# Transposing k and q by DMA instead of on TensorE, from the sixth slot on, in a linear-attention kernel fused with a bilinear FFN

## The chip, the core and the metric

The kernel runs on one core of a Trainium2 chip. The core has TensorE (PE, with its weight loads shown apart as PEld), VectorE (DVE), ScalarE (ACT), GpSimd (POOL) and SyncE (SP); each engine works through its own list of instructions in order, and 16 DMA engines serve the transfers that SP and ACT issue. The metric is the device time of one execution in microseconds (us), less is better.

## What is computed

q, k and v are 4 batches x 8 heads x 768 positions x 64 (float32). A state of 64 x 64 for each head is decayed by gamma and gets the outer product of k and v at each position; y is q times the state. Then y, laid out as 3072 tokens x 512, goes through a bilinear feed-forward layer with three weights of 512 x 1536, 512 x 1536 and 1536 x 512.

```python
for t in range(S):
    state = gamma[None, :, None, None] * state + np.einsum('bhd,bhe->bhde', k[:, :, t], v[:, :, t])
    y[:, :, t] = scale * np.einsum('bhd,bhde->bhe', q[:, :, t], state)
...
a = x @ w_a
b = x @ w_b
return (a * b @ w_out).astype(np.float32)
```

## The kernel before, in words

**Slots.** The 3072 tokens are 24 slots of 128 (4 batches x 6 chunks). The recurrence is done in its chunked form: within a slot as masked attention, between the slots of a batch by a state that PE accumulates in PSUM. A slot passes through these steps:

- `load_slot` (line 81): three DMAs from SP, 256 KB each, for k, q and v in float32. The buffers `kf`, `qf`, `vf` are six deep. Weights are loaded by `load_w` and `load_o` (768 KB each) from the same queue. `LOADS` (line 19) is the order of all loads; the first five are issued at once, the rest in line 306.
- `casts` (line 166): k is multiplied by a decay table into `kb` (bf16), q into `qb`, v is cast to `vb`. From slot 3 on all three run on POOL. These buffers are six deep too.
- `step_a` (line 178): eight PE transposes of 128 x 128 (lines 181 and 183) put k and q into one PSUM tile, and a DVE copy (line 185) brings them to SBUF as `kqT`, three deep.
- `step_b` (line 187): eight matmuls `at` (line 193) from `kqT`, the mask on DVE (line 197, into `aT`), the state update `st` (line 203), and two ACT copies of the state.
- `step_c` (line 212): the output `y` of the slot, from the state and `kqT` (line 218) and from `vb` and `aT` (line 223), copied by ACT into `xt` (line 228).

**FFN.** Slots are grouped in seven tiles J of 3, 2, 4, 4, 4, 4 and 3 slots. `ffn_ab` (line 246) makes one of twelve blocks of the hidden layer of a tile: four matmuls `a` (line 253), an ACT cast, four matmuls `g` (line 259), and a product on DVE (line 261). `ffn_out` (line 263) makes the 128 x 512 output of one slot with twelve matmuls `o` (line 266), an ACT copy, and a store issued from the ACT queue.

**Order.** `seq` (line 70) chains every instruction to the one before on its engine, so that the order in the code is the order on each engine. `run` (line 273) lays the steps of the next tile between the FFN pieces of this one, at positions that are given as a list, in the order a, (c of the slot before), b; it issues the casts of a slot up to four pieces ahead. The first FFN tile starts when slots 0 to 2 are through. During J=1, slots 5 to 8 are done: the pieces are the last six `ffn_ab` of J=1, then the three `ffn_out` of J=0 and two of J=1, and the positions (line 317) put step a of slot 5 before the fourth of these pieces and step b of slot 5 before the fifth.

**Waits of DMAs.** The transfers use eight semaphores in turn: a DMA issue waits for the transfer that used its semaphore last, so no more than eight are under way at a time, stores of the ACT queue among them. An issue waits in its queue, and what stands behind it waits too.

Of the kernel before, what the change touches and what calls it, by code (L numbers as in the profile page):

```python
# [10 lines left out]
BF16 = mybir.dt.bfloat16  # L11
# [6 lines left out]

LOADS = ("s0 s1 s2 w0 w1 s3 w2 s4 w3 o0 o1 o2 o3 "
         + " ".join(f"s{t}" for t in range(5, 24))).split()  # L20


@with_exitstack
def kernel(
# [10 lines left out]
    nc = tc.nc  # L35
    P = 128
    B, H, S, D = q.shape
    NCH = S // P
    HP = H // 2
# [4 lines left out]
    NSLOT = B * NCH  # L44
# [9 lines left out]
    wstage = ctx.enter_context(tc.tile_pool(name="wstage", bufs=4))  # L54
    raw = ctx.enter_context(tc.tile_pool(name="raw", bufs=6))
    nat = ctx.enter_context(tc.tile_pool(name="nat", bufs=6))
    tra = ctx.enter_context(tc.tile_pool(name="tra", bufs=3))
    xtp = ctx.enter_context(tc.tile_pool(name="xtp", bufs=2))
    asbp = ctx.enter_context(tc.tile_pool(name="asbp", bufs=3))
    htp = ctx.enter_context(tc.tile_pool(name="htp", bufs=2))  # L60
# [9 lines left out]
    def seq(bi):  # L70
        ins = bi.ins
        prev = last.get(ins.engine)
        if prev is not None:
            tc.add_manual_dep(ins, prev.name, nosync, reason="program order")
        last[ins.engine] = ins
        return bi
# [25 lines left out]
    pending = list(LOADS)  # L102

    def issue_loads(n):
        for _ in range(min(n, len(pending))):
            what = pending.pop(0)
            {"s": load_slot, "w": load_w, "o": load_o}[what[0]](int(what[1:]))
# [33 lines left out]
    def cast(engine, dst, src):  # L141
        if engine is nc.scalar:
            seq(nc.scalar.copy(dst, src))  # L143
        else:
            seq(engine.tensor_copy(dst, src))  # L145
# [10 lines left out]
    kb, qb, vb, kqT, aT = {}, {}, {}, {}, {}  # L156
# [9 lines left out]
    def casts(t):  # L166
        ci = t % NCH
        early = t < TILES[0]
        kb[t] = nat.tile([P, H, D], BF16, tag="kb", name="kb")
        qb[t] = nat.tile([P, H, D], BF16, tag="qb", name="qb")  # L170
        vb[t] = nat.tile([P, H, D], BF16, tag="vb", name="vb")
        seq((nc.vector if early else nc.gpsimd).tensor_tensor(  # L172
            kb[t], raws["k", t], ktab[:, ci, :, :].to_broadcast([P, H, D]), op=ALU.mult))
        seq(nc.gpsimd.tensor_tensor(  # L174
            qb[t], raws["q", t], qtab[:, ci, :, :].to_broadcast([P, H, D]), op=ALU.mult))
        cast(nc.scalar if early else nc.gpsimd, vb[t], raws["v", t])

    def step_a(t):
        tp = psat.tile([P, 2, HP, P], BF16, tag="at", name="tp")
        for hp in range(HP):  # L180
            seq(nc.tensor.transpose(tp[:, 0, hp, :], kb[t][:, 2 * hp : 2 * hp + 2, :], ident))  # L181
        for hp in range(HP):
            seq(nc.tensor.transpose(tp[:, 1, hp, :], qb[t][:, 2 * hp : 2 * hp + 2, :], ident))  # L183
        kqT[t] = tra.tile([P, 2, HP, P], BF16, tag="kqT", name="kqT")
        seq(nc.vector.tensor_copy(kqT[t], tp))  # L185

    def step_b(t):
# [24 lines left out]
    def step_c(t):  # L212
        ci = t % NCH
        J, i = where[t]
        y = psat.tile([P, HP, P], F32, tag="at", name="y")
        if ci > 0:
            for hp in range(HP):
                seq(nc.tensor.matmul(y[:, hp, :], gst[t % 2][:, hp, :], kqT[t][:, 1, hp, :],  # L218
                                     start=(hp == 0), stop=False, skip_group_check=True))
        for hp in range(HP):  # L220
            for e in range(2):
                r = slice(64 * e, 64 * e + 64)
                seq(nc.tensor.matmul(y[r, hp, :], vb[t][:, 2 * hp + e, :], aT[t][:, e, hp, :],  # L223
                                     start=(ci == 0 and hp == 0), stop=(hp == HP - 1),
                                     skip_group_check=True))
        if i == 0:
            xt[J] = xtp.tile([P, KT, 4 * P], BF16, tag="xt", name="xt")
        seq(nc.scalar.copy(xt[J][:, :, i * P : (i + 1) * P], y))  # L228

    def steps(slots):  # L230

        slots = list(slots)
        todo = []
        for i in range(len(slots) + 1):
            if i < len(slots):
                todo.append((step_a, slots[i]))
            if i > 0:
                todo.append((step_c, slots[i - 1]))
            if i < len(slots):
                todo.append((step_b, slots[i]))  # L240
        return todo
# [32 lines left out]
    def run(work, todo, at, ahead=4):  # L274

        order = []
        for g, w in enumerate(work):
            order += [todo[i] for i in range(len(todo)) if at[i] == g]
            order.append(w)
        starts = [s for fn, s in todo if fn is step_a]  # L280
        for i, (fn, *args) in enumerate(order):
            for fn2, *a2 in order[i : i + ahead + 1]:
                if fn2 is step_a and a2[0] in starts:
                    starts.remove(a2[0])
                    casts(a2[0])
            fn(*args)

    def ab0(ft):
# [4 lines left out]
    casts(0)  # L293
    casts(1)
    step_a(0)
    casts(2)
    step_b(0)
    step_a(1)
    step_c(0)
    step_b(1)  # L300
# [2 lines left out]
    step_b(2)  # L303
    cast_w(0)
    step_c(2)
    issue_loads(100)

    work = [(ab0, ft) for ft in range(NFT)] + [(ffn_ab, 1, ft) for ft in range(6)]
    todo = steps([3, 4])
    run(work, todo, [6, 7, 9, 10, 11, 12], ahead=3)  # L310
    for j in range(NW):
        cast_o(j)
    work = [(ffn_ab, 1, ft) for ft in range(6, NFT)]
    work += [(ffn_out, 0, i) for i in range(TILES[0])]
    work += [(ffn_out, 1, i) for i in range(TILES[1])]
    todo = steps(range(5, 9))
    run(work, todo, [3, 4, 5, 6, 6, 7, 7, 8, 8, 9, 9, 10])
    slot = sum(TILES[:3])
    for J in range(2, len(TILES)):
        n = TILES[J]  # L320
        nxt = range(slot, slot + TILES[J + 1]) if J + 1 < len(TILES) else range(0)
        slot += len(nxt)
        todo = steps(nxt)
        work = [(ffn_ab, J, ft) for ft in range(NFT)] + [(ffn_out, J, i) for i in range(n)]
        run(work, todo, [i * (len(work) - 1) // len(todo) for i in range(len(todo))])
# [30 lines left out]
```

## Time and profile before

| | us |
|---|---|
| median of 3 runs (255.37 to 256.64) | 256.04 |
| the profiled execution, its time | 255.94 |
| its span in the trace | 254.2 |
| PE busy | 233.5 |
| DVE busy | 102.2 |
| ACT busy | 91.6 |
| POOL busy | 73.6 |
| loads on the SP queue, share of 16 DMA engines | 50.1% |
| stores on the ACT queue, share of 16 DMA engines | 6.7% |

The span is 1.7 us shorter than the time of that execution; a change of the span is taken to change the time by as much. The profile has a view of the span in 40 slices, a chain of work that ended last (from the last instruction back to whatever released each piece), groups of instructions by line, DMA issues with their time to landing, and the order of instructions in time. In the chain a matmul counts only until the next one starts, so that its times add up; in the groups the durations of matmuls overlap.

### The profile page before, as it was taken

The page shows a single profiled execution, that of the slowest core. Times are in us where ns is not written, and L with a number is a line of the kernel's source. Part 1 is how long each engine was busy: PE and PEld are TensorE (multiplying, and loading weights), DVE is VectorE, ACT ScalarE, POOL GpSimd, SP SyncE. Part 2 cuts the span into 40 slices and gives each one's busy share as a digit, 9 for nine tenths or more (in the row PEclk, how much of TensorE's full clock was granted, in tenths as well). Part 3 has the DMA queues.
Part 4 walks back from the last instruction along what each step waited for, and adds up shares of the span by engine and source line. Part 5 has one row for each costly group of instructions (what it writes and reads, how often), then busy time and mean ns, then how long its engine had stood idle before and what let it go on. Part 6 is the DMA issues. An engine that isn't in the chain of part 4 may idle for free.

```text
span 254.2 us, 4303 instructions
## 1 busy us (share of the span) xinstructions
PE 233.5 (92%) x1672; PEld 127.0 (50%) x1696; DVE 102.2 (40%) x173; ACT 91.6 (36%) x179; POOL 73.6 (29%) x84
## 2 busy tenths in 40 slices
PE   0487889899999999999999999999999999999994
PEld 0363445786555455445455445445445454446641
DVE  1462375465325456305455306455205465104410
ACT  2154233534243442423434412444314333223311
POOL 5115474286757667503133403000000000000000
PEclk9999999999999999999999999999999999999999
DMA  7999997999999999969910021000021000120012
GB/s 155 219 358 289 303 292 257 296 217 205 252 239 271 209 214 220 191 173 274 183 32 3 3 112 55 0 0 3 24 100 44 0 0 3 41 97 27 3 41 84
DMA packets 84181, 34.88 MB, mean 137 GB/s; under 512 B 75457, under 2 KB 79553, under 8 KB 84161
## 3 DMA queue, kind: packets, MB, share of 16 engines
q1 hardware_dynamic: 80704, 28.32, 50.1%
q10 hardware_dynamic: 3456, 6.29, 6.7%
q8 instruction: 13, 0.21, 0.4%
q14 instruction: 8, 0.06, 0.1%
HBM read 28.31 MB, written 6.29 MB: 136 GB/s over the span
## 4 chain that ended last, share of the span: by engine, by line
PE 88%; SPq 3%; DMA 2%; ACT 2%; DVE 2%; issue 2%; DVEq 0%; ACTq 0%
PE g L259 25%; PE a L253 25%; PE o L266 24%; PE y L223 3%; PE at L193 3%; SPq L86 3%; PE st L203 3%; DMA vf<-in_v_dram 2%; PE tp L181 2%; PE tp L183 2%; PE y L218 2%; DVE wb_bf L145 1%; ACT gst L210 1%; ACT wa_bf L143 1%; ACT xt L228 0%
## 5 line engine op out<-in xcount | busy, mean ns | idle before, releaser
L261 DVE TENSOR_TENSOR ht<-g,asb 128x512 bf16<-128x512 f32 (+2 forms) x84 | 51.6, 615 | 86.8 <-PE g L259 69.2
L253 PE MATMUL a<-xt,wa_bf 128*128 128x512 bf16 (+2 forms) x325 | 76.6, 354 | 2.7 <-ACT xt L228 2.3
L259 PE MATMUL g<-xt,wb_bf 128*128 128x512 bf16 (+2 forms) x332 | 76.5, 353 | 2.6 <-DVE wb_bf L145 2.5
L256 ACT CAST asb<-a 128x512 bf16<-128x512 f32 (+2 forms) x84 | 44.0, 524 | 70.6 <-PE a L253 56.1
L266 PE MATMUL o<-wo_bf,ht 128*128 128x512 bf16 x279 | 63.5, 379 | 0.6 <-issue 0.2
L259 PEld LDWEIGHTS <-wb_bf 128*128 128x128 bf16 x336 | 33.0, 99 | 33.5 <-DVE wb_bf L145 3.6
L266 PEld LDWEIGHTS <-ht 128*128 128x128 bf16 x288 | 27.4, 98 | 31.6
L253 PEld LDWEIGHTS <-wa_bf 128*128 128x128 bf16 x336 | 30.7, 99 | 24.6 <-issue 2.7
L197 DVE TENSOR_TENSOR aT<-at,mask 128x512 bf16<-128x512 f32 x48 | 30.7, 681 | 7.0 <-PE at L193 7.0
L172 POOL TENSOR_TENSOR kb<-kf,ktab 128x512 bf16<-128x512 f32 x21 | 21.9, 1042 | 37.0 <-DMA kf<-in_k_dram 16.7
L185 DVE COPY kqT<-tp 128x1024 bf16<-128x1024 bf16 x24 | 16.4, 683 | 38.4 <-PE tp L183 38.4
L269 ACT COPY osb<-o 128x512 f32<-128x512 f32 x24 | 14.0, 585 | 46.7 <-PE o L266 36.7
L174 POOL TENSOR_TENSOR qb<-qf,qtab 128x512 bf16<-128x512 f32 x24 | 25.0, 1042 | 11.7 <-DMA qf<-in_q_dram 11.2
L210 ACT CAST gst<-st 64x256 bf16<-64x256 f32 x40 | 14.6, 366 | 15.5 <-PE st L203 15.1
L228 ACT CAST xt<-y 128x512 bf16<-128x512 f32 x24 | 14.0, 585 | 15.9 <-PE y L223 13.4
L145 POOL CAST vb<-vf 128x512 bf16<-128x512 f32 x21 | 13.5, 644 | 20.9 <-issue 14.9
L181 PE MATMUL tp<-ident,kb 128*128 128x128 bf16 x96 | 10.0, 230 | 5.0 <-DVE kb L172 5.0
L223 PE MATMUL y<-aT,vb 128*64 128x128 bf16 x192 | 11.1, 235 | 2.1 <-DVE aT L197 2.1
L193 PE MATMUL at<-kqT 64*128 64x128 bf16 x192 | 10.2, 230 | 2.5 <-DVE kqT L185 2.0
L181 PEld LDWEIGHTS <-kb 128*128 128x128 bf16 x96 | 7.7, 103 | 9.1 <-DVE kb L172 5.0
L193 PEld LDWEIGHTS <-kqT 64*128 64x128 bf16 x192 | 5.8, 98 | 10.5 <-issue 7.1
L183 PE MATMUL tp<-ident,qb 128*128 128x128 bf16 x96 | 10.0, 231 | 0.9 <-POOL qb L174 0.9
(28 smaller groups left out, 68.0 us busy)
## 6 DMA issues: line engine op xcount, KB each, us to landing
kf<-in_k_dram SPq DMA_DIRECT2D x24, 256.0 KB, 5.1
qf<-in_q_dram SPq DMA_DIRECT2D x24, 256.0 KB, 5.1
vf<-in_v_dram SPq DMA_DIRECT2D x24, 256.0 KB, 5.1
out_dram<-osb ACTq DMA_DIRECT2D x24, 256.0 KB, 2.1
wsta<-in_moe_w_a_dram SPq DMA_DIRECT2D x4, 768.0 KB, 6.5
wstb<-in_moe_w_b_dram SPq DMA_DIRECT2D x4, 768.0 KB, 7.6
wsto<-in_moe_w_out_dram SPq DMA_DIRECT2D x4, 768.0 KB, 7.3
```

Of the source, the lines that this page charges most:

```text
L172: seq((nc.vector if early else nc.gpsimd).tensor_tensor(kb[t], raws["k", t], ktab[:, ci, :, :].to_broadcast([P, H, D]), op=ALU.mult))
L174: seq(nc.gpsimd.tensor_tensor(qb[t], raws["q", t], qtab[:, ci, :, :].to_broadcast([P, H, D]), op=ALU.mult))
L181: seq(nc.tensor.transpose(tp[:, 0, hp, :], kb[t][:, 2 * hp : 2 * hp + 2, :], ident))
L193: seq(nc.tensor.matmul(at[e][:, hp, :], kqT[t][r, 0, hp, :], kqT[t][r, 1, hp, :], start=True, stop=True))
L197: seq(nc.vector.tensor_tensor(aT[t][:, e], at[e], mask, op=ALU.mult))
L210: seq(nc.scalar.copy(g[r, :, r], st[r, :, r]))
L223: seq(nc.tensor.matmul(y[r, hp, :], vb[t][:, 2 * hp + e, :], aT[t][:, e, hp, :], start=(ci == 0 and hp == 0), stop=(hp == HP - 1), skip_gr ...
L253: seq(nc.tensor.matmul(a, wa_bf[:, kt, fs], xt[J][:, kt, :w], start=(kt == 0), stop=(kt == KT - 1)))
L256: seq(nc.scalar.copy(asb, a))
L259: seq(nc.tensor.matmul(g, wb_bf[:, kt, fs], xt[J][:, kt, :w], start=(kt == 0), stop=(kt == KT - 1)))
L261: seq(nc.vector.tensor_tensor(ht[J][:, ft, :w], g, asb, op=ALU.mult))
L266: seq(nc.tensor.matmul(o, ht[J][:, ft, i * P : (i + 1) * P], wo_bf[:, ft, :], start=(ft == 0), stop=(ft == NFT - 1)))
```

## The change

`step_a` of slots 5 to 23 no longer transposes on PE. It issues two DMA transposes from the SP queue, one from `kb` and one from `qb`, straight into the two halves of `kqT`: bf16, 128 x 512 each, 128 KB. The PE transposes, the PSUM tile and the DVE copy of these slots go. Slots 0 to 4 stay as they were. The buffers `kqT` and `aT` become four deep. The slot loads are no longer all issued in line 306: those of slots 9 to 23 are held back, and one slot's load is issued with the casts of each slot from 5 on.

In the program this gives the following order on the SP queue after the weights. L5 stands for the three loads of slot 5, T5 for its two transposes: L5 L6 L7 L8 L9 L10 T5 T6 L11 L12 T7 T8 L13 L14 T9 T10 L15 T11 L16 T12 L17 L18 T13 T14 L19 T15 L20 T16 L21 L22 T17 T18 L23 T19 T20 T21 T22 T23. Each T of k waits for the cast of k and for the last reader of its `kqT` buffer, which is step c of the slot four before; each T waits for the cast that makes its source. The first matmul of step b waits for both T of its slot.

```diff
+DMA_FROM = 5
...
-    tra = ctx.enter_context(tc.tile_pool(name="tra", bufs=3))
+    tra = ctx.enter_context(tc.tile_pool(name="tra", bufs=4))
...
     def step_a(t):
+        kqT[t] = tra.tile([P, 2, HP, P], BF16, tag="kqT", name="kqT")
+        if t >= DMA_FROM:
+            for i, src in enumerate((kb[t], qb[t])):
+                seq(nc.sync.dma_start_transpose(kqT[t][:, i], src.rearrange("p h d -> p (h d)")))
+            return
         tp = psat.tile([P, 2, HP, P], BF16, tag="at", name="tp")
         for hp in range(HP):
             seq(nc.tensor.transpose(tp[:, 0, hp, :], kb[t][:, 2 * hp : 2 * hp + 2, :], ident))
         for hp in range(HP):
             seq(nc.tensor.transpose(tp[:, 1, hp, :], qb[t][:, 2 * hp : 2 * hp + 2, :], ident))
-        kqT[t] = tra.tile([P, 2, HP, P], BF16, tag="kqT", name="kqT")
         seq(nc.vector.tensor_copy(kqT[t], tp))
...
                 if fn2 is step_a and a2[0] in starts:
                     starts.remove(a2[0])
                     casts(a2[0])
+                    if a2[0] >= DMA_FROM:
+                        issue_loads(1)
...
-    issue_loads(100)
+    issue_loads(len(pending) - (NSLOT - 9))
```

## The prediction

> **What bounds the kernel now.** I read the page's head, the slices and the chain first.
>
> ```profile
> span 254.2 us, 4303 instructions
> ...
> PE 233.5 (92%) x1672; PEld 127.0 (50%) x1696; DVE 102.2 (40%) x173; ACT 91.6 (36%) x179; POOL 73.6 (29%) x84
> ...
> DMA  7999997999999999969910021000021000120012
> ...
> PE 88%; SPq 3%; DMA 2%; ACT 2%; DVE 2%; issue 2%; DVEq 0%; ACTq 0%
> ```
>
> PE is the bound: 88% of the chain. But for the first 20 slices (6.36 us each, so until about 127 us) the DMA engines are as full as PE. Two limits lie side by side there, and the change moves work from one to the other. So the stage to look at is where slots 5 to 8 pass, 52 to 80 us. The chain of that stretch (start, duration, what):
>
> ```profile
> 55.12 0.22 PE tp L181 x4
> 55.34 0.22 PE tp L183 x4
> 55.57 0.44 PE a L253 x4
> 56.00 0.44 PE g L259 x4
> 56.44 0.33 PE at L193 x8
> ...
> 66.37 0.33 PE at L193 x8
> ...
> 77.60 0.86 PE a L253 x4
> ...
> 79.33 0.33 PE at L193 x8
> ```
>
> A slot's eight transposes hold PE for 0.22 + 0.22 = 0.44 us. Step b of slots 5, 7 and 9 (the `at` rows) starts at 56.44, 66.37 and 79.33, and tile J=2 begins at 77.60. PE has no gap here. The loads for these slots, from the SP queue's order in time (start, length of the issue), and POOL's casts:
>
> ```profile
> 50.61 0.94 SPq L86 DMA_DIRECT2D kf<-in_k_dram  x1
> ...
> 61.76 1.07 SPq L86 DMA_DIRECT2D kf<-in_k_dram  x1
> ...
> 68.51 0.88 SPq L86 DMA_DIRECT2D vf<-in_v_dram  x1
> ```
>
> ```profile
> 53.18 1.04 POOL L174 TENSOR_TENSOR qb<-qf,qtab 128x512 bf16<-128x512 f32 x1
> ...
> 64.43 1.04 POOL L174 TENSOR_TENSOR qb<-qf,qtab 128x512 bf16<-128x512 f32 x1
> ...
> 70.72 1.04 POOL L172 TENSOR_TENSOR kb<-kf,ktab 128x512 bf16<-128x512 f32 x1 [0.40 <-PE y L223]
> ```
>
> From slot 6's k (50.61) to slot 9's k (61.76) nine loads are issued, 1.24 us each: this is the pace of a full queue. Slot 5's q is cast by 54.2, slot 8's q is cast at 64.43, slot 10's k at 70.72, each soon after it landed. So before, slots 5 to 8 get their data just in time, with PE transposing within about a microsecond of the cast.
>
> **What the change removes.** 19 slots x 0.44 us = 8.4 us from PE, all on the chain. It also takes 19 copies of 683 ns from DVE; DVE is 40% busy and waits for PE, so that is worth nothing. The fourth `kqT`/`aT` buffer costs nothing.
>
> **What it adds: T5 stands behind the loads of slots 9 and 10.** Step b of slot 5 needs T5, at 56.44 - 0.44 = 56.0. T5 comes after L10 in the queue. First bound, the issue: T5 of k waits for the semaphore last used by the eighth transfer before it, slot 8's q, in use until about 64.4 (its cast); T5 of q waits for slot 8's v (cast at 65.5). So they can't even be issued before 64 and 65.5. Second, the engines: if the transfers of one queue are served in order, T5 moves after L10. Slot 10's k lands at about 70.6, q and v follow at 1.2 each: 73.0. Then two transposes, x each. T5 is there at 73.0 + 2x.
>
> **What is x?** No row shows a DMA transpose. From below: 128 KB at the 250 GB/s of this stage is 0.5 us. Next, a whole load's pace, 1.2 us, for twice the bytes. Next, a store, the only transfer out of SBUF that the trace has, lands in 2.1 us; that is x if transposes don't overlap each other. From above, a load's landing in the full queue, 5.1 us.
>
> ```profile
> kf<-in_k_dram SPq DMA_DIRECT2D x24, 256.0 KB, 5.1
> ...
> out_dram<-osb ACTq DMA_DIRECT2D x24, 256.0 KB, 2.1
> ```
>
> A transpose scatters each source row over all partitions, so I take no less than a load, and between 1.2 and 2.1 the nearer side of the load: **x = 1.5**. Both ends, 0.5 and 5.1, stay for the range.
>
> [...]
>
> **The sum at x = 1.5.**
> 1. T5 at 76.0 against 56.0: PE stands for 20.0 us in front of step b of slot 5. Nothing hides it: all that follows on PE, the `ffn_out` of J=0 too, stands behind that matmul.
> 2. After such a stop PE starts slowly. At the first FFN tile, after little work on PE, the first 16 matmuls take 1.44 + 3 x 1.28 = 5.3 us, where four soon take 0.65 (2.6 for 16). I charge 2.7 us, though the granted clock is 1.00 in these windows and I can't say that the same will come.
>
> ```profile
> 21.54 1.44 PE a L253 x4
> 22.98 1.28 PE g L259 x4
> 24.26 1.28 PE a L253 x4
> 25.54 1.28 PE g L259 x4
> ...
> 31.33 0.65 PE g L259 x4
> ```
>
> 3. T7 comes after T6, L11, L12: T5 + 2x + 6 x 1.2 + 2x and 0.7 for a store between (6.7% of 254.2 us over 24 stores), T5 + 13.9. Step b of slot 7 is wanted at T5 + (66.37 - 56.44) - 0.88 (two slots' transposes) + 2.7 = T5 + 11.75. 2.15 us are lost. T6, at T5 + 3.0, is early enough: step b of slot 6 is due at T5 + 5.5.
> 4. T9 comes after T8, L13, L14: T5 + 13.9 + 3.0 + 7.2 + 3.0 + 2.8 (four stores) = T5 + 29.9. Step b of slot 9 is wanted at T5 + 13.9 + (79.33 - 66.37) - 0.88 = T5 + 26.0. 3.9 us are lost.
> 5. From there the queue gains: a slot costs DMA 3.0 + 3.7 + 0.7 = 7.4 us, and PE about 9.4 (tile J=3 begins at 115.35 in the chain, 37.7 us after J=2, four slots). T(t) waits for step c of slot t-4, about three slots, 28 us, ahead of its use; the loads behind it in the queue are ten slots ahead. Stores share the eight semaphores, so an ACT store can wait for a transpose, and ACT's copies behind it; with this lead it doesn't. I charge nothing; were DMA slower than PE per slot (x above 2.5), this cover is gone.
>
> Together 20.0 + 2.7 + 2.15 + 3.9 - 8.4 = +20.35: 255.94 + 20.35 = 276.3, **276 us** (the median of the runs is 0.1 above the profiled execution; I add nothing).
>
> By the same steps x = 0.5 gives 18.0 + 2.7 - 8.4 = +12.3, 268; x = 2.4 gives 21.8 + 2.7 + 5.75 + 7.5 - 8.4 = +29.35, 285.
>
> **Rivals.**
> - *Transposes are the bound* (x of 2.5 to 5.1). For it: scattered small pieces. Against: half the bytes of a load. At x = 3 the steps give 291 (slot 6 is late by 0.5 as well), and each of some ten slots costs 1.0 more than PE takes: about 301. At 5.1 DMA is the bound to the end: 38 x 5.1 + 13 slots' loads at 3.7 + 16 stores at 0.7 = 253 after 73.0, and 40 us from the last `at` (213.9) to the end: a span of 366, 368.
> - *Transposes overtake the loads.* If T5 is bound by its issue alone, it lands some 2 us (a store's landing) after 65.5, at 67.5: 11.5 - 8.4 = +3.1 without the slow start, +5.8 with it: 259 to 262. Against it: the loads of one queue land in order throughout.
> - *The other side: faster.* The stop at slot 5 is cheaper than 8.4 us. With the slow start the turn is at T5 = 56.0 + 8.4 - 2.7 = 61.7. For that the 18 loads from 45.2 on would have to be through by about 60, 0.8 us each instead of 1.24, and the issue's bound of 64 would have to fall. With no stop left it gives 255.94 - 8.4 = 247.5. Speaking for it: weight loads in the slices before run at up to 358 GB/s. Against it: where slot loads make the traffic, the windows from 46 to 115 us show 212 to 255.
> - *The change doesn't do what it says*: the transposes stay. Not so: the program has 304 fewer rows on PE, 19 x 16 transposes with their weight loads.
>
> **Chances.** T5 behind the loads, x up to 2.5 (264 to 287): 0.64, and 276 is near its middle. Transposes as the bound, above 287: 0.20. Overtaking, 258 to 264: 0.08. Faster by over 0.5% (about what a measurement can tell): 0.05. Within 0.5%: 0.03. The range takes in the case of the early T5's upper end and the slow transposes up to x = 3 and a little: 262 to 305. The further tail to 368 stays out.
>
> **What would show it.** A gap of about 20 us on PE before the first `at` of slot 5, released by DMA, from 56 on; the DMA slices full through it; step a's rows 96 - 76 = 20 left in each of its two groups; smaller gaps before slots 7 and 9, none later; the transposes' landing time. The forecast is wrong if T5 lands well before slot 10's v, or if gaps before `at` recur in every slot to the end.

## The result, and the profile after

The changed kernel takes 270.87 us (median of 4 runs, 270.1 to 271.21) against 256.34 (4 runs of the kernel before, 255.37 to 257.11): a ratio of 1.056, 95% interval 1.052 to 1.059. The forecast was 276, range 262 to 305. The profiled execution took 270.68 us, 14.7 more than that of before. The page of the changed kernel first: the engines, the slices, and the first DMA queue (packets, MB, share of 16 engines).

```profile
span 269.0 us, 4032 instructions
...
PE 227.8 (85%) x1523; PEld 119.4 (44%) x1544; DVE 90.3 (34%) x154; ACT 91.7 (34%) x179; POOL 72.7 (27%) x84
...
PE   1487888910096999999999999999999999999994
...
PEclk9997999995579799999999999999999999999999
DMA  8999997999999999998999474211021100020002
...
q1 hardware_dynamic: 101376, 33.30, 59.8%
```

PE does less (227.8 us against 233.5) and the span is longer. The hole is in slices 9 to 11 of the PE row, 54 to 74 us, with the DMA row full beneath it, and the granted clock (PEclk) falls in the same place. From the queue's row the price of a transpose can be had: (59.8% of 269.0 - 50.1% of 254.2) / 38 = 0.88 us of packet time on all 16 engines. Who waited on PE from 54 us on, in the view of waits (total, times, longest):

```profile
PE at L201 <- DMA kqT<-qb: 20.5, 2, 18.4
```

Two waits for a transpose, in front of step b of slots 5 and 7, and none after. In PE's order in time (start, length, in brackets the idle time before and its releaser):

```profile
53.97 0.60 PE L261 MATMUL a<-xt,wa_bf 128*128 128x256 bf16 x4
54.41 0.60 PE L267 MATMUL g<-xt,wb_bf 128*128 128x256 bf16 x4
73.36 0.61 PE L201 MATMUL at<-kqT 64*128 64x128 bf16 x8 [18.35 <-DMA kqT<-qb]
...
86.41 0.40 PE L201 MATMUL at<-kqT 64*128 64x128 bf16 x8 [2.16 <-DMA kqT<-qb]
```

And SP's order in time shows why T5 is so late: its casts were done by 54.5, but it is issued at 68.4, right behind the last load of slot 10, and the loads in front of it go out one by one, some 1.2 us apart.

```profile
67.16 1.14 SPq L90 DMA_DIRECT2D vf<-in_v_dram  x1
68.41 1.76 SPq L186 DMA_TRANSPOSE kqT<-kb  x1
70.27 1.21 SPq L186 DMA_TRANSPOSE kqT<-qb  x1
```

In the chain tile J=2 begins at 98.49 in place of 77.60, 20.9 us late:

```profile
98.49 0.86 PE a L261 x4
```

From there to the end the span is 6.1 us shorter than before: 14 slots x 0.44 = 6.2.

### The profile page after: what moved, and what is told of

It reads as the page before. It is cut to its first block, busy times and chain, and to the rows that moved or that the text cites. A ratio compares the mean times of both kernels' runs of the same rounds, so it can differ in the third digit from the quotient of the medians.

```text
span 269.0 us, 4032 instructions
## 1 busy us (share of the span) xinstructions
PE 227.8 (85%) x1523; PEld 119.4 (44%) x1544; DVE 90.3 (34%) x154; ACT 91.7 (34%) x179; POOL 72.7 (27%) x84
## 3 DMA queue, kind: packets, MB, share of 16 engines
q1 hardware_dynamic: 101376, 33.30, 59.8%
## 4 chain that ended last, share of the span: by engine, by line
PE 63%; SPq 16%; DMA 13%; issue 2%; ACT 2%; POOL 2%; ACTq 0%; POOLq 0%
PE o L274 19%; PE a L261 18%; PE g L267 18%; SPq L90 14%; DMA vf<-in_v_dram 5%; DMA wsto<-in_moe_w_out_dram 4%; PE y L231 2%; PE at L201 2%; PE st L211 2%; DMA qf<-in_q_dram 2%; DMA kf<-in_k_dram 2%; DMA kqT<-qb 1%; PE y L226 1%; SPq L97 1%; SPq L186 1%
## 5 line engine op out<-in xcount | busy, mean ns | idle before, releaser
L267 PE MATMUL g<-xt,wb_bf 128*128 128x512 bf16 (+2 forms) x334 | 77.6, 356 | 2.6 <-DVE wb_bf L149 2.4
L274 PE MATMUL o<-wo_bf,ht 128*128 128x512 bf16 x279 | 65.4, 386 | 0.7 <-issue 0.4
L261 PEld LDWEIGHTS <-wa_bf 128*128 128x128 bf16 x336 | 31.6, 100 | 28.5 <-issue 2.4
L176 POOL TENSOR_TENSOR kb<-kf,ktab 128x512 bf16<-128x512 f32 x21 | 21.9, 1042 | 43.9 <-DMA kf<-in_k_dram 26.1
L201 PE MATMUL at<-kqT 64*128 64x128 bf16 x192 | 10.4, 233 | 22.6 <-DMA kqT<-qb 20.5
L178 POOL TENSOR_TENSOR qb<-qf,qtab 128x512 bf16<-128x512 f32 x24 | 25.6, 1065 | 9.2 <-DMA qf<-in_q_dram 7.6
L149 POOL CAST vb<-vf 128x512 bf16<-128x512 f32 x21 | 12.8, 611 | 34.1 <-PE y L231 14.6
L218 ACT CAST gst<-st 64x256 bf16<-64x256 f32 x40 | 14.7, 367 | 15.8 <-PE st L211 15.4
L231 PE MATMUL y<-aT,vb 128*64 128x128 bf16 x192 | 10.9, 232 | 2.1 <-DVE aT L205 2.1
L231 PEld LDWEIGHTS <-vb 128*64 128x64 bf16 x192 | 6.6, 113 | 6.1 <-issue 4.2
L211 PE MATMUL st<-vb,kb 128*128 128x128 bf16 x80 | 8.6, 234 | 0.5 <-ACT gst L218 0.5
L226 PEld LDWEIGHTS <-gst 128*128 128x128 bf16 x80 | 6.5, 103 | 3.9
L226 PE MATMUL y<-kqT,gst 128*128 128x128 bf16 x80 | 8.2, 228 | 0.0
## 6 DMA issues: line engine op xcount, KB each, us to landing
kf<-in_k_dram SPq DMA_DIRECT2D x24, 256.0 KB, 4.8
qf<-in_q_dram SPq DMA_DIRECT2D x24, 256.0 KB, 5.0
vf<-in_v_dram SPq DMA_DIRECT2D x24, 256.0 KB, 5.1
out_dram<-osb ACTq DMA_DIRECT2D x24, 256.0 KB, 2.2
```

Source lines behind the costliest of these rows:

```text
L176: seq((nc.vector if early else nc.gpsimd).tensor_tensor(kb[t], raws["k", t], ktab[:, ci, :, :].to_broadcast([P, H, D]), op=ALU.mult))
L178: seq(nc.gpsimd.tensor_tensor(qb[t], raws["q", t], qtab[:, ci, :, :].to_broadcast([P, H, D]), op=ALU.mult))
L201: seq(nc.tensor.matmul(at[e][:, hp, :], kqT[t][r, 0, hp, :], kqT[t][r, 1, hp, :], start=True, stop=True))
L261: seq(nc.tensor.matmul(a, wa_bf[:, kt, fs], xt[J][:, kt, :w], start=(kt == 0), stop=(kt == KT - 1)))
L267: seq(nc.tensor.matmul(g, wb_bf[:, kt, fs], xt[J][:, kt, :w], start=(kt == 0), stop=(kt == KT - 1)))
L274: seq(nc.tensor.matmul(o, ht[J][:, ft, i * P : (i + 1) * P], wo_bf[:, ft, :], start=(ft == 0), stop=(ft == NFT - 1)))
```

## The experiments

The theory is called "place in the queue": all of the loss comes from where T5 to T8 stand in SP's order, behind loads that nobody needs yet. The rivals: transposes are too dear for the full DMA engines; they are late wherever they stand; the loads that are held back are late. Every run is compared with the kernel before, timed beside it (255.9 to 256.4).

### 1. Transposes from slot 9 on, each behind the next load only

```diff
-DMA_FROM = 5
+DMA_FROM = 9
...
                 seq(nc.sync.dma_start_transpose(kqT[t][:, i], src.rearrange("p h d -> p (h d)")))
+            issue_loads(1)
             return
...
-                    if a2[0] >= DMA_FROM:
-                        issue_loads(1)
...
-    issue_loads(len(pending) - (NSLOT - 9))
+    issue_loads(len(pending) - (NSLOT - 11))
```

> Slots 5 to 8 go back to TensorE, slots 9 to 23 stay with DMA; each transpose stands in the queue behind the load of the next slot only (L9 L10 T9 L11 T10 L12 T11 ...). Theory 'place in the queue': the loss is the two stops in front of slots 5 and 7, because T5 stands behind L10 and T7 behind L12. Here T9 is there at about 74.5 + 1.8 = 76.3 us, before its use at 79, and no stop is left: 255.9 - 15 x 0.44 = 249.3 us, PE with no wait for a transpose over 0.5 us. Rival 'the engines can't take it' (transposes cost DMA time that the loads need, until 130 us): T9 to T12 run in the same full queue as T5 to T8 did, so stops of some us come back in J=2: 256 us or more. Rival 'late whatever the place': a transpose takes too long from cast to use, 255 or more.

Measured: 249.29 us (4 runs, 249.06 to 249.38), ratio 0.974 (0.973 to 0.976). This is the best kernel of the study, 2.6% faster than the one before and 8% faster than the changed one. All PE waits from 60 us to the end, and SP's rows around T9:

```profile
PE o L275 <- issue: 0.2, 1, 0.2
```

```profile
68.15 0.72 SPq L90 DMA_DIRECT2D vf<-in_v_dram  x1
71.94 1.28 SPq L186 DMA_TRANSPOSE kqT<-kb  x1
73.33 1.21 SPq L186 DMA_TRANSPOSE kqT<-qb  x1
```

T9 is issued by 74.5; step b of slot 9 starts at 79.04 and waits for nothing. The gain is 6.65 us, 15 x 0.44. The DMA engines were about as full here in J=2 as in the changed kernel's stop (DMA share 1.10 from 74 to 112 us against 1.13 from 54 to 74; it is the sum of the packets' times over 16 engines' time, and packets overlap, so it can pass 1). So both rivals fall as they were put: the transposes of slots 9 to 23 stood early enough in this run, and PE waited for none of them in the full stage.

### 2. T5 three slot loads earlier

```diff
-    issue_loads(len(pending) - (NSLOT - 9))
+    issue_loads(len(pending) - (NSLOT - 6))
```

> The changed kernel with one number altered: loads are held back from slot 6 on, not 9, so that T5 stands behind L7, three slot loads earlier (L5 L6 L7 T5 T6 L8 L9 T7 T8 L10 L11 T9 ...). 'Place in the queue': three loads are 11.1 us, T5 lands at 73.3 - 11.1 = 62.2, the first stop falls from 18.4 to about 7 us, and the time by about 11 us, to 260. 'The engines can't take it' and 'late whatever the place': the first stop stays within 3 us of 18 and the time at 268 to 271.

Measured: 259.0 us (2 runs, 258.86 and 259.13). PE's rows with an idle time in front of a step b:

```profile
61.97 0.61 PE L201 MATMUL at<-kqT 64*128 64x128 bf16 x8 [6.12 <-DMA kqT<-qb]
74.74 0.40 PE L201 MATMUL at<-kqT 64*128 64x128 bf16 x8 [1.13 <-DMA kqT<-qb]
...
88.14 0.40 PE L201 MATMUL at<-kqT 64*128 64x128 bf16 x8 [1.28 <-DMA kqT<-qb]
```

The first stop falls from 18.35 to 6.12 us, T5 comes 11.4 us earlier, and the time falls by 11.9. One number moves the loss as the theory says. Small stops remain in front of slots 7 and 9; T5 still stands behind L6 and L7.

### 3. Only slots 5 to 8 by DMA

```diff
-        if t >= DMA_FROM:
+        if DMA_FROM <= t < 9:
```

> Only slots 5 to 8 are transposed by DMA, 9 to 23 on TensorE, the order of the loads as in the changed kernel. 'Place in the queue': all of the loss sits in slots 5 to 8 and each later slot only gained 0.44 us, so the time rises by 15 x 0.44 = 6.6 us to 277.5, with the two stops of 18.4 and 2.2 us unchanged. Rival 'the later transposes cost too': without them the time falls below 270.9.

Measured: 275.1 us (274.82 and 275.38). The two stops were not unchanged but 16.65 and 1.45 us, 2.4 us less than in the changed kernel:

```profile
72.71 0.61 PE L201 MATMUL at<-kqT 64*128 64x128 bf16 x8 [16.65 <-DMA kqT<-qb]
...
85.46 0.40 PE L201 MATMUL at<-kqT 64*128 64x128 bf16 x8 [1.45 <-DMA kqT<-qb]
```

270.87 + 6.6 - 2.4 = 275.1. That this comes out so well is partly luck: PE reached slot 5 about 1.0 us later here (56.1 against 55.0), and after the shorter second stop the granted clock stayed at 1.00, which saves the 1.7 us of a second slow start; the two pull opposite ways. Even so, slots 9 to 23 earned their 0.44 us each in the changed kernel too, and the loss is in slots 5 to 8.

### 4. Only the hold-back of the loads

```diff
-        if t >= DMA_FROM:
+        if t >= NSLOT:
```

> No DMA transpose at all: TensorE transposes every slot, but the slot loads are held back and the buffers are four deep as in the changed kernel. 'Place in the queue' holds that the hold-back alone costs nothing, since the loads keep their order and run ten slots ahead: within 0.5% of 256. Rival 'the loads are late': over 258, with POOL waiting for slot loads and PE for POOL.

Measured: 256.0 us (10 runs, 255.19 to 256.43), ratio 0.9999 (0.9985 to 1.0013). Holding the loads back, and the fourth buffers, cost nothing by themselves that these runs could tell.

### 5. Slots 5 to 8 from the ACT queue

Run 3 with one word changed.

```diff
-                seq(nc.sync.dma_start_transpose(kqT[t][:, i], src.rearrange("p h d -> p (h d)")))
+                seq(nc.scalar.dma_start_transpose(kqT[t][:, i], src.rearrange("p h d -> p (h d)")))
```

> Only slots 5 to 8 by DMA, as in the run that had only these, but issued from the ACT queue in place of the SP queue; so they stand behind no load, while the 16 DMA engines carry the same bytes. 'Place in the queue': T5 is issued right after the cast of slot 5's q (54.4 us), lands 3 to 4 us later at 58 to 59, and the first stop falls from 17 to 3 or 4 us. The later ones may be stops of 1 to 3 us each, since ACT now issues each transpose just ahead of its use; time 258 to 270 against 275.1. Rival 'the engines are full': T5 shares them with the same loads, so that it still lands at 66 or later; a first stop of 11 us or more.

Measured: 275.65 us (275.01 and 276.29), as slow as run 3. The sizes that I gave were wrong: a first stop of 7.84 us lies between the 3 or 4 of the theory and the 11 of the rival. PE's and ACT's rows:

```profile
54.32 2.76 ACTq L186 DMA_TRANSPOSE kqT<-kb  x1
...
57.18 1.28 ACTq L186 DMA_TRANSPOSE kqT<-qb  x1
...
63.38 0.61 PE L201 MATMUL at<-kqT 64*128 64x128 bf16 x8 [7.84 <-DMA kqT<-qb]
...
73.66 0.61 PE L201 MATMUL at<-kqT 64*128 64x128 bf16 x8 [6.05 <-DMA kqT<-qb]
...
83.39 0.56 PE L201 MATMUL at<-kqT 64*128 64x128 bf16 x8 [1.97 <-DMA kqT<-qb]
```

T5 is there 9.3 us earlier than in run 3 (63.4 against 72.7), so the place in SP's order did hold it back; but it still took 6.2 us from the second issue to its use, not 3 to 4. The shortest landing of a transpose here is 2.4 us, the median 5.2; from the SP queue in run 3, at a DMA share of 1.29 from 68 to 72 us and 1.32 from 77 to 83, the median is 3.8. That the full engines are part of the price here is my estimate; no run shows it apart from the change of queue. The gain was lost again: ACT can issue T6 only when it gets there in its own order, so T6 comes just in front of its use (6.05 us), and SP's loads now wait for semaphores that the transposes hold, 12.9 us in one piece:

```profile
SPq L90 <- DMA kqT<-kb: 17.4, 3, 12.9
```

### 6. Each transpose from slot 13 on twice

Run 1 with this edit:

```diff
-                seq(nc.sync.dma_start_transpose(kqT[t][:, i], src.rearrange("p h d -> p (h d)")))
+                for _ in range(2 if t >= 13 else 1):
+                    seq(nc.sync.dma_start_transpose(kqT[t][:, i], src.rearrange("p h d -> p (h d)")))
```

> The kernel with transposes from slot 9 on and the load of the next slot between, with each DMA transpose of slots 13 to 23 issued twice (the second writes the same again): 22 transposes more. The first profiles give a transpose 0.88 us of all 16 engines (extra time of the SP queue's packets over 38, and over 30). 'Place in the queue' with the lead that these slots have: the time stays at 249.3 within 0.5%, and the queue's packets take 22 x 0.88 = 19 us more. Rival 'a transpose's own price': 5 to 20 us longer, with PE waiting for transposes in J=3 and after.

Measured: 268.03 us (4 runs, 265.92 to 268.17), ratio to the kernel before 1.043 (1.038 to 1.049); 18.7 more than run 1. The queue's packets took 65.3% of 266.2 - 62.1% of 247.6 = 20.1 us more, 0.91 for a transpose, as expected; the time is not. But the run had a fault of mine: the second transpose writes what the first wrote, so SP waits until the first has landed, and its queue with it.

```profile
SPq L187 <- DMA kqT<-kb: 28.4, 11, 3.6
SPq L187 <- DMA kqT<-qb: 14.8, 11, 2.6
```

These 43 us of waiting, and the 11.0 us that PE in turn waited for transposes in five stops, are not the transposes' own price, and the run settles nothing about that price.

### 7. The second transposes into a buffer of their own

Run 1 with this edit:

```diff
                 seq(nc.sync.dma_start_transpose(kqT[t][:, i], src.rearrange("p h d -> p (h d)")))
+                if t >= 13:
+                    dup = tra.tile([P, HP, P], BF16, tag="dup", name="dup")
+                    seq(nc.sync.dma_start_transpose(dup, src.rearrange("p h d -> p (h d)")))
```

> The run with doubled transposes again, but the second transpose of each pair writes a buffer of its own (nobody reads it), so it needs not wait for the landing of the first. In the run before, SP waited 43 us for the landing of the first of each pair. Theory 'a wait for landing in SP's order was the price, not the transposes': the time falls from 268.0 to 249.3 within 1% (two more issues of 1.2 us a slot, inside 9.4 us), with the same 19 to 20 us more of queue time. Rival 'the transposes' own price': 262 or more, with PE stops in J=3 and after.

Measured: 258.53 us (10 runs, 256.8 to 260.06), ratio 1.008 (1.005 to 1.011). Half of the way back from 268.0, and 9.2 more than run 1: both expectations missed. No step b waits for a transpose in this profile, whose time is 256.80. The stop is elsewhere. In PE's waits:

```profile
PE g L271 <- ACT osb L281: 5.6, 1, 5.6
```

ACT's order in time around it, with ACT's store issues (ACTq):

```profile
140.65 0.59 ACT L281 COPY osb<-o 128x512 f32<-128x512 f32 x1 [1.85 <-PE o L278]
148.18 0.40 ACTq L283 DMA_DIRECT2D out_dram<-osb  x1
148.62 0.59 ACT L240 CAST xt<-y 128x512 bf16<-128x512 f32 x1 [7.38 <-DMA vf<-in_v_dram]
149.10 0.59 ACT L281 COPY osb<-o 128x512 f32<-128x512 f32 x1
155.30 0.34 ACTq L283 DMA_DIRECT2D out_dram<-osb  x1
155.69 0.59 ACT L281 COPY osb<-o 128x512 f32<-128x512 f32 x1 [5.99 <-DMA qf<-in_q_dram]
```

The copy for a store is done at 141.2, the store goes out at 148.18, once a slot load of v has landed; the next waits from 149.7 to 155.30 for a slot load of q. The store has no business with these loads: it uses the semaphore that they used last. Behind the store stand ACT's copies, which free PSUM for PE. The stop of 5.6 us, and a granted clock of 0.72 from 148 to 160 us, make up most of the 7.5 us by which this execution is longer than run 1's. The queue had fallen behind: SP issues these two loads at 143.95 and 151.03, and in run 1 the same two at 131.44 and 139.06, 12 us earlier. The DMA share is 1.02 from 95 to 133 us, and SP's issues of a slot take about 8 us of PE's 9; which of the two holds the queue back is not shown. The transposes themselves kept a lead (T13 to T16 landed 11 to 15 us ahead of their use), so their price does count here, but it came through the stores and not through `at`. Whether the same doubling from slot 17 on, past the full stretch, would be free was not measured.

### 8. PE kept busy in the first stop

```diff
     def step_b(t):
         ci = t % NCH
+        if t == DMA_FROM:
+            warm = psat.tile([P, 2, HP, P], BF16, tag="at", name="warm")
+            for _ in range(300):
+                seq(nc.tensor.transpose(warm[:, 0, 0, :], vb[t][:, 0:2, :], ident))
```

> The changed kernel with 300 PE transposes, whose result nobody reads, ahead of step b of slot 5; at 55 ns each they fill 16.5 of the 18.4 us in which PE waits for T5. Theory of the slow start: after the stop PE ran at a granted clock of 0.51 for 3.9 us, where 16 matmuls of 256 columns took 3.3 us in place of 1.7. With PE busy until shortly before, the clock stays up and the time falls by about 1.7 us, to 269.2; the second stop keeps its own slow stretch (granted 0.65 for 4.9 us). Rival: the slow stretch has another cause (the DMA traffic): 270.9 or more, and the clock at 0.5 after T5 again.

Measured: 272.13 us (4 runs, 271.77 to 273.42), ratio to the kernel before 1.062 (1.057 to 1.068). The clock did as expected, the time did not. The columns are those of the view by stretches; after the length come the engines' busy times, then the granted clock, DMA share and GB/s. The changed kernel, from T5's arrival to the end of the second slow stretch:

```profile
73.30:77.20 3.90, 3.84 (x24) 2.75 (x25) 1.71 (x3) 0.75 (x2) 0.01 (x1) 0.51 0.56 122
77.20:84.20 7.00, 6.95 (x57) 3.36 (x56) 1.71 (x3) 2.49 (x5) 4.78 (x5) 1.00 1.27 215
84.20:86.40 2.20, 0.04 (x1) 0.02 (x1) 0.00 (x0) 0.59 (x1) 0.61 (x1) 1.00 1.05 264
86.40:91.30 4.90, 4.67 (x24) 2.12 (x26) 1.29 (x2) 0.73 (x2) 1.04 (x1) 0.65 0.98 213
```

This run, the same places:

```profile
75.60:78.00 2.40, 2.40 (x28) 2.02 (x28) 1.67 (x4) 0.74 (x2) 0.08 (x1) 1.00 0.46 93
78.00:84.70 6.70, 6.65 (x53) 3.14 (x52) 1.67 (x3) 2.49 (x5) 3.29 (x4) 1.00 1.23 223
84.70:87.80 3.10, 0.01 (x1) 0.00 (x0) 0.00 (x0) 0.59 (x1) 2.10 (x3) 1.00 1.24 285
87.80:92.70 4.90, 4.70 (x24) 2.17 (x26) 1.29 (x2) 0.73 (x2) 0.28 (x1) 0.65 0.73 160
```

At full clock PE is 1.8 us faster through the first two stretches (1.5 and 0.3), and stands 0.9 us longer in front of slot 7: T7 comes when the queue brings it. So about half of the slow start after the first stop is hidden by the second stop. That T5 came 2.2 us later than in the changed kernel (75.6) makes the rest. That delay arose in the queue, not before it: SP issued slot 6's k at the same time in both (50.74 here, 50.79 there), but T5's second transpose at 71.81 in place of 70.27. Why is open; run 9 asks.

### 9. The same with fewer, wider matmuls

```diff
-            warm = psat.tile([P, 2, HP, P], BF16, tag="at", name="warm")
-            for _ in range(300):
-                seq(nc.tensor.transpose(warm[:, 0, 0, :], vb[t][:, 0:2, :], ident))
+            warm = psat.tile([P, HP * P], F32, tag="at", name="warm")
+            for _ in range(75):
+                seq(nc.tensor.matmul(warm, vb[t][:, 0:2, :], wa_bf[:, 0, : HP * P], start=True, stop=True))
```

> The changed kernel with 75 matmuls of 512 columns (0.216 us each, 16.2 us, result not read) in the stop before step b of slot 5, in place of 300 transposes: 150 PE instructions in place of 600. The slow start is gone again (granted clock 1.00 after T5). If many small PE instructions made T5 land 1 to 2 us later, it lands as in the changed kernel, and the time is 270.9 - 1.7 = 269.2. If what delays T5 is PE being busy at all, or if the time before slot 5 just differs from run to run, it stays at 271 to 272.

Measured: 270.78 us (5 runs, 270.42 to 273.83), the same as the changed kernel. Of T5's delay it settles nothing: from the issue of slot 6's k to step b of slot 5 it is 22.6 us in the changed kernel, 23.2 in run 3, 23.4 here and 24.9 in run 8, so run 3, with PE idle, lies as late as this one. Nor was the slow start gone, as I had expected: PE idled for 2.7 us between the filling and T5, and the half clock came about 1.2 us after the restart, at 76.2.

## Why the prediction was right, and where its sizes were off

The direction, the place and the mechanism were right: the working's step 1 is the loss. Going through its steps, in the profiled executions:

1. **T5 behind L10.** Forecast at 76.0, a stop of 20.0 us; PE went on at 73.36 after 18.35. L10's last load landed at 72.2 (issued at 67.16, 5.0 to landing), a little sooner than reckoned (73.0). What was mis-sized is **x**: 1.5 was taken, and a transpose takes 0.88 us of the engines; T5 landed 1.0 us after L10 and not 3.0, less than the 1.76 us of its two transposes, so its packets must have moved while the last load was still landing.
2. **The slow start**, charged at 2.7 with a doubt: it came, at a granted clock of 0.51, and cost 1.7 us on PE (step b's `at` and the 16 matmuls behind it in 3.86 us where before took 2.19). The doubt was about the rows of the first FFN tile; in the changed kernel's trace the granted clock of that tile is 0.50 from 22.52 to 25.90, where its rows are 1.28 us apart too, so the slow rows of before are likely of the same kind. In run 8 about half of what the full clock won was lost again to the wait for T7. It came a second time after the stop of 2.16 us, which the working had not charged: the twelve matmuls of an `ffn_out` took 4.3 us in place of 2.6. That one is not hidden by any later wait.
3. **T7**, forecast 2.15 us late: 2.16. The agreement is partly luck. T7 came 13.05 us after T5 (forecast 13.9) and was wanted after 10.9 (forecast 11.75). With x at 0.88 the same sum gives 11.4, so the queue lost 1.6 us that the sum doesn't have. The profile suggests where: SP took 5.9 us, from 68.41 to 74.32, to issue the four transposes of T5 and T6, which are 3.5 us of work for the engines, and the DMA share fell to 0.56 from 73.3 to 77.2. No run tests this.
4. **T9**, forecast 3.9 us late: not late, but only just. Its second transpose was issued at 94.39 and landed 5.1 later, at 99.5; step b of slot 9 started at 100.15 with no wait. T9 was there 26.1 us after T5 in place of 29.9, and wanted after 26.8 in place of 26.0. Of the 3.8 us, 2.9 lie between T7 and T9, where four transposes at 0.88 in place of 1.5 give 2.5.
5. **From there the queue gains**: right for PE (no wait for a transpose after slot 7), with a lead that was thinner than the text says: T10 landed about 8 us ahead of its use, T13 14, and the 28 us came only at T20. Nor are the loads ten slots ahead: in SP's order L15 stands right in front of T11, and L23 in front of T19. In J=3's start a store of ACT waited for a slot load in the changed kernel, and the chain of work runs through it:

```profile
129.59 7.03 DMA vf<-in_v_dram
...
137.13 0.59 ACT asb L264
...
137.77 0.38 PE g L267
```

It cost PE next to nothing there, but it is the mechanism that run 7 turned into 5.6 us. "With this lead it doesn't" was wrong.

**The 0.44 us for a slot** held: 6.65 us for 15 slots in run 1. The sum: forecast +20.35, measured +14.74. From the first to the second: stop of slot 5 -1.65, first slow start -1.0 (1.7 for 2.7), T7 0, T9 -3.9, second slow start +1.7, and -1.0 because PE reached slot 5 1.0 us earlier in this execution, before any DMA transpose (at 55.0 in place of 56.0). That gives 14.5.

The rival "transposes are the bound" is out: 0.88 is below its 2.5. "Overtaking" is out as well: T5 landed behind L10. "Faster" came true for another choice of slots and another placement only, run 1.

## What to carry to other kernels

When work moves from a compute engine to a DMA queue, look first at where it stands in that queue's order and what is in front of it; the bytes come second. Here transposes of slots 5 to 23 gave +5.6%, with the first of them behind loads that nobody needed yet, and those of slots 9 to 23 gave -2.6%, where the queue was ahead of its use. In a stage where the DMA engines are full, move only the work that can stand ahead of its use by more than a landing takes there (5.2 us in the median for a transpose in run 5); and see which other transfers share the semaphores: in run 7, with the queue 12 us late, two stores waited until 148.18 and 155.30 us for slot loads, and PE stood for 5.6 us.

## What the runs showed of the hardware

- A DMA transpose of 128 x 512 in bf16 (128 KB, SBUF to SBUF) took 0.88 to 0.91 us of packet time on all 16 engines, 544 packets ((101376 - 80704) / 38), about 1.2 us to issue on SP, and landed in 2.4 us at best, 3.1 in the median. A slot load of twice the bytes went at 1.24 us in the full queue before.
- A stop of 2.16 us was enough to bring TensorE to a granted clock of 0.65 over the next 4.9 us; stops of 1.04 and 1.11 us (run 9) were followed by full speed. A stop of 2.69 us in run 8 passed without a drop, while one of 2.68 us in run 9 was followed by half clock. The view by stretches shows what differs. In the first 100 us of the changed kernel the granted clock changed at 22.52, 25.93, 60.07, 77.14, 87.38 and 90.79 us, each a whole number of steps of 3.41 us after the one before. Behind the stop of 2.16 us it was at 0.50 for one such step and at 1.00 on both sides of it:

```profile
83.97:87.38 3.41, 1.25 (x16) 0.69 (x15) 0.56 (x1) 0.79 (x2) 0.81 (x2) 1.00 1.08 251
87.38:90.79 3.41, 3.19 (x8) 1.21 (x8) 0.73 (x2) 0.53 (x2) 0.66 (x1) 0.50 0.93 199
90.79:94.20 3.41, 3.41 (x35) 1.91 (x34) 1.29 (x2) 1.80 (x4) 2.17 (x4) 1.00 1.20 220
```

PE was busy for 1.25 us of the step before the drop. In the step that ends where the clock drops, it was busy for 1.16 us in run 9 (72.79 to 76.20; a granted clock of 0.82 from 73 to 78 us puts the drop there) and 1.44 in run 5 (80.07 to 83.48, a stop of 1.97, behind which `at` took 0.56 us in place of 0.40). The 2.69 us of run 8 fell across the end of a step, by an estimate that counts its steps of 3.41 us back from its next drop, at about 88.33: PE was busy for 1.63 us of 71.27 to 74.68 and 2.49 of the next, and the clock stayed at 1.00. So in these runs the drop goes with the busy time within a step, and not with the length of the stop alone; no run was made to vary it.
- ACT's queue: 6.2 us from the issue of a transpose to its use (run 5). The other queue took T5 past the loads that stood in front of it (9.3 us earlier), but its transposes landed in 5.2 us in the median, against 3.8 from SP's queue in run 3; the cause was not shown.
